# Start bytes of the on-chip buffers in a fused attention, mixing and channel kernel

## The chip, the cores and the metric

The kernel runs on one core of a Trainium2 chip, as one program. The metric is the device time of one execution in microseconds (us). The engines are TensorE (PE, with its weight loads PEld), VectorE (DVE), ScalarE (ACT), GpSimd (POOL) and the queue of SyncE (SP), which issues all DMAs.

## The reference

Three stages follow each other, with batch 4, 576 positions and 512 channels.

```
attention: 8 heads of 64; heads 0-3 see a window of 32, heads 4-7 every 4th of 128 positions
x  = softmax(mask(q k^T / 8)) v                          # (4, 576, 512)
xk = mu_k x + (1 - mu_k) x_prev;  xr = mu_r x + (1 - mu_r) x_prev   # x_prev: one position back
y  = sigmoid(xr w_r) * (relu(xk w_k)^2 w_v)              # w_k: 512x1024, w_v: 1024x512
u  = y + (y^T U V)^T                                     # U: 576x32, V: 32x576, over positions
out = u + relu(u w_ch1) w_ch2                            # w_ch1: 512x2048, w_ch2: 2048x512
```

## The kernel before

All products of the second and third stage are made with channels on the 128 partitions. A float32 operand is split in two (`hi_lo`, `part_split`): ACT copies it rounded into a high half, DVE or POOL subtracts to get the low half. A product is then a trio of float32r matmuls: high weights times high data, low weights times high data, high weights times low data. In a matmul the first operand named in a row of the profile is the one that streams through the array (the moving operand), the second is the one that is loaded before it (the stationary operand, here always the weights).

**Mixing stage.** The 2304 positions are cut into 8 chunks of 288 columns (`HS`). Chunk 0 uses plain float32 matmuls (lines 1101 and 1116) while the weights still come in. Chunks 1 to 7 use trios (lines 1088 to 1090), with data in the tiles `xk` (tag `A`) and `k2s` (tag `B`) and weights in pieces of 128x512 (tag `w`, 42 of them, names `wh` and `wl`). Attention for later chunks runs between them: small matmuls (lines 848, 913, 949, 1005), softmax on DVE, ACT and POOL with the small tiles `mn` and `sm` (tags with 3 buffers), and `x_out`, which writes the attention's output into tile `x`, one row of 577 columns for each of four channel blocks (column 0 holds a zero, for `x_prev`).

**Channel stage.** From about 332 us on, the last two products run in groups of 512 columns by a seven-product scheme (`ch1`, `ch2`), in blocks of 256 columns (`Q`). Old tiles get new tenants ("boxes"): the data `u` and its sums stand in the tags `w64` and `raw` (profile names `boxw` and `boxraw`), the hidden values' high halves in `B`, `raw` and the end of `x`, their low halves in the two buffers of `x`: `x[0]` for even steps `j`, `x[1]` for odd ones. The weights of three steps in four (`j % 4 < 3`) stand in pieces of tag `w`, those of the fourth in the boxes `A` and `B`. Matmuls of `ch1` are lines 1365 to 1367, those of `ch2` lines 1453 to 1455. DVE makes the sums, the low halves, the weights' sums for later steps and the stores' sums.

**Order.** Each engine's order comes from a planner (`plan`): it walks over all operations by fixed ranks (`RANKS`) and assumed durations, and lets an operation that opens a new buffer of a tag wait for the buffer's previous tenant (`x.bufs`). The order is fixed when the program is built.

**Where the buffers lie.** `Lazy` asks the pool for a tile when an operation first uses it. A pool gives each tag one stretch, in the order of first use; each buffer of a tag is rounded up to a multiple of 32 bytes. The small pool `cp` starts at a multiple of 128 bytes, with `cst_t` (1792 bytes in each partition), `mu_t` (32) and `zero` (2048); the big pool follows. So the start bytes, modulo 128, are:

| tag, in order | buffers x bytes | starts at byte (of 128) |
|---|---|---|
| raw | 4 x 5120 | 32 |
| x | 2 x 9232 (9248) | 32 and 64 |
| w64 | 4 x 4096 | 96 |
| pr | 4 x 2560 | 96 |
| mn, sm | 3 x 20 (32) each | 96, 0, 32; 64, 96, 0 |
| w32 | 3 x 2048 | 32 |
| w | 42 x 2048 | 32 |
| pt, d, sig, rt, B, m, A, y, k2, us, vs | all multiples of 128 | 32 |

A chunk's 288 columns take 1152 bytes, a block's 256 columns 1024 bytes: both are multiples of 128, so each operand inside a tile starts at the same byte of 128 as its tile. In tile `x` a row takes 2308 bytes, so its four rows start 4 bytes apart.

Of the kernel before, what the change touches and what calls it, by code (L numbers as in the profile page):

```python
# [12 lines left out]
F32 = mybir.dt.float32  # L13
# [7 lines left out]
B, H, S, D = 4, 8, 576, 64  # L21
DM, DFF, DCH, RANK = 512, 1024, 2048, 32
P = 128
HS = S // 2
NCH = 2 * B
NPAIR = H // 2
# [25 lines left out]

NPIECE = 42
XW = 16 * HS

CLAMP = 400
END_ENG = ("ACT",) * 8 + ("DVE",)
# [146 lines left out]
def tile_attention_mix_channel(  # L204
# [4 lines left out]
    cp = ctx.enter_context(tc.tile_pool(name="cp", bufs=1))  # L209
    pool = ctx.enter_context(tc.tile_pool(name="pool", bufs=2))  # L210
# [4 lines left out]
    cst_t = cp.tile([P, P + NALL * KW], F32, name="cst_t")  # L215
    ident = cst_t[:, 0:P]
    masks = [cst_t[:, P + i * KW : P + (i + 1) * KW] for i in range(NALL)]
    mu_t = cp.tile([P, 8], F32, name="mu_t")
    zero = cp.tile([P, CW], F32R, name="zero")

    def f32(ap):
# [1 line left out]


    ops = []

    class Lazy:

# [5 lines left out]
        def __call__(self):  # L234
            if self.real is None:
                shape, dt, name = self.args
                self.real = self.home.tile(shape, dt, tag=self.tag, name=name, bufs=self.bufs)
            return self.real

    def bank(tag):  # L240

        return Lazy([P, 512], F32, tag, f"ps{tag}", 4, ps)
# [4 lines left out]
    def op(eng, ns, fn, r=(), w=(), more=100, lock=False, mode=None, size=0):  # L247

        o = Op()
        o.eng, o.ns, o.fn, o.r, o.w, o.more, o.lock, o.mode, o.size = eng, ns, fn, list(r), list(w), more, lock, mode, size  # L250
        ops.append(o)
# [227 lines left out]
    def dma(nbytes, fn, r, w):  # L479
        op("SP", 415, fn, r, w, size=nbytes)  # L480
# [13 lines left out]
    def copy(n, out_, in_, r, w, psum=False, strided=False):  # L494
        act(n, lambda: nc.scalar.activation(out_(), in_(), AF.Copy), r, w, psum, strided)  # L495
# [244 lines left out]
    xt = {}  # L740
    raws = {}

    def unit(u):
        part_i, pair = divmod(u, NPAIR)
        b, part = divmod(part_i, 2)
        return b, part, pair
# [65 lines left out]
    def x_out(ov, q, part, b):  # L812

        if b not in xt:
            xt[b] = Lazy([P, NPAIR, S + 1], F32, "x", f"x{b}", 2)
            op("POOL", 105, lambda: nc.gpsimd.memset(xt[b]()[:, :, 0:1], 0.0), [], [(xt[b], "z")])
        t0, t1 = PARTS[part]

        def dst():
            d = xt[b]()[:, q, 1 + t0 : 1 + t1]  # L820
            return d.rearrange("p (m r) -> p r m", r=DIL) if q >= NPAIR // 2 else d

        def src():
            s_ = ov()[:, : t1 - t0]
            return s_.rearrange("p (r m) -> p r m", r=DIL) if q >= NPAIR // 2 else s_

        copy(t1 - t0, dst, src, [(ov,)], [(xt[b], q, part)], psum=True, strided=q >= NPAIR // 2)

    def attend(u):
# [3 lines left out]
        b, part, pair = unit(u)  # L833
# [1 line left out]
        raw = raws.pop(u)  # L835
        sc = [bank("M" if u < SC_M else "S") for _ in range(2)]
        pr = Lazy([P, 10 * KW], F32, "pr", "pr", 4)
        mn, sm = Lazy([P, 5], F32, "mn", "mn", 3), Lazy([P, 5], F32, "sm", "sm", 3)
        pt, ov = bank("S"), bank("S")
        pts = Lazy([P, 5 * P], F32, "pt", "pts", 2)  # L840

# [76 lines left out]
        pe(nw * 4, nw * 2 * 66, pv, [(pts, 0), (raw, "v")], [(ov,)], "pv")  # L918
        yield
        x_out(ov, pair, part, b)  # L920
        yield

    def attend2(ua, ub):
# [4 lines left out]
        b, part, pair = unit(ua)  # L928
# [1 line left out]
        rq, rv = raws.pop(("qk", ua // 2)), raws.pop(("v", ua // 2))  # L930
        sc = [bank("S") for _ in range(2)]
        pr = Lazy([P, 10 * KW], F32, "pr", "pr", 4)
        mn = [Lazy([P, 5], F32, "mn", "mn", 3) for _ in range(2)]
        sm = [Lazy([P, 5], F32, "sm", "sm", 3) for _ in range(2)]
        pt, ov = bank("S"), [bank("S") for _ in range(2)]
        pts = Lazy([P, 5 * P], F32, "pt", "pts", 2)
        ns = nw // 2
# [74 lines left out]
        for x in range(2):  # L1012
            x_out(ov[x], pair + x, part, b)
# [36 lines left out]
    k20 = Lazy([P, 8 * HS], F32, "B", "k20", 1)  # L1050
    xk = Lazy([P, XW], F32R, "A", "xk", 1)
    k2s = Lazy([P, XW], F32R, "B", "k2s", 1)

# [143 lines left out]
    yb = {}  # L1197
# [3 lines left out]
    uacc = {}  # L1201

    def load_y(b):
        yb[b] = Lazy([P, NPAIR, S + 1], F32, "x", "yb", 2)
        dma(P * S * 16, lambda: nc.sync.dma_start(yb[b]()[:, :, :S], ytmp[b]),
            [("y", b, o, h) for o in range(4) for h in range(2)], [(yb[b],)])

# [377 lines left out]
    def fresh(n):  # L1585

        nonlocal nunit
        us_ = range(nunit, min(nunit + n, NU))
        nunit += len(us_)
        for d in (0, 2):  # L1590
            for what in ("qk", "v"):
                for u in us_ if d == 0 or nunit > NPAIR else ():
                    fetch(u + d, what)
        return [attend2(*us_)] if len(us_) == 2 else [attend(u) for u in us_]
# [33 lines left out]
    for p in range(NPAIR):  # L1628
        mix(0, p, "k")
    divided = 0  # L1630
    side = [lambda: load_y(0)] + uv_u(0, "S", "S") + uv_v(0, "S") + uv_v(1, "S") + [lambda: load_y(1)]
    side += uv_u(1, "S", "S") + uv_v(2, "S") + uv_v(3, "S")
    side += [lambda: load_y(2)] + uv_u(2, "S", "S") + uv_v(4, "S") + uv_v(5, "S")
    for c in range(NCH - 1):
        cur = quanta(c) if c else first
# [34 lines left out]
    for n, (g, j0, j1) in enumerate(VISITS):  # L1670
        boxes.pop(("sig", 0), None)
        nxt = x_steps(VISITS[n + 1][0]) if n + 1 < len(VISITS) else []
        todo = [lambda: load_y(3)] + uv_u(3, "S", "S") + uv_v(6, "S") + uv_v(7, "S") if n == 0 else []
        each = (len(todo) + 3) // 4
        for j in range(j0, j1):
            hid = ch1(g, j)
            for what in LATER.get((n, j), ()):
                prep(*what)
            if PRESUM <= 4 * n + j < PRESUM + 8:
                presum(4 + (4 * n + j - PRESUM) // 2, 1 + (4 * n + j - PRESUM) % 2)  # L1680
            for _ in range(each):
                if todo:
                    todo.pop(0)()
            if prev is not None:
                ch2(*prev)
            prev = (g, j, hid, j == j0, j == j1 - 1, (j0 == 0, j1 == 8))
            for fn in nxt[:1] if j == (j0 if j1 - j0 == 4 else j1 - 2) else nxt[1:] if j == j1 - 1 else ():
                fn()
# [106 lines left out]
```

## Time and profile before

| | |
|---|---|
| median of 3 runs | 725.76 us (725.61 to 726.69) |
| profiled execution | 726.45 us, of which the span from first to last instruction is 724.6 us |
| PE busy | 715.0 us (99%) |
| DVE busy | 596.3 us (82%) |
| ACT busy | 422.8 us (58%) |
| POOL busy | 128.1 us (18%) |
| PE's share of the chain that ended last | 89% |

Busy is the time in which at least one instruction of an engine runs, waits inside PE's pipeline included, so a busy PE isn't one at its peak. The chain that ended last is followed back from the last instruction, at each step to what released it.

### The profile page before, as it was taken

The numbers are of one execution on the slowest core, as the hardware profiler recorded it, in microseconds if no ns is written. First come the engines' busy times: TensorE is split into PE (matmuls) and PEld (weight loads), VectorE is DVE, ScalarE is ACT, GpSimd is POOL, SyncE is SP. The second block draws the span as 40 slices with busy tenths as digits, with TensorE's granted clock in tenths as the row PEclk, the third lists the DMA queues.
The fourth block names the chain that finished last, engine by engine and source line by source line (L and its number), as shares of the span: only waits on it lengthen the run. The fifth ranks groups of instructions, "written<-read, shape, count | busy, mean of one in ns | idle before, by whom it ended". The sixth has DMA issues, their size and how long they took to land.

```text
span 724.6 us, 19178 instructions
## 1 busy us (share of the span) xinstructions
PE 715.0 (99%) x7534; PEld 692.9 (96%) x7534; DVE 596.3 (82%) x1526; ACT 422.8 (58%) x1047; POOL 128.1 (18%) x164
## 2 busy tenths in 40 slices
PE   8999999999999999999899999999999999999997
PEld 6778999999999999999899999999999999999997
DVE  5879988687767645899998999999999898897853
ACT  5887886867676835275643544445586445444321
POOL 0101364646463724130000000000000000000000
PEclk9999999999999999999999999999999999999999
DMA  8986257676647430756546446442554213103221
GB/s 318 350 276 233 83 190 264 234 265 229 233 149 265 156 122 1 252 171 210 188 125 205 142 144 209 153 140 74 164 185 133 59 57 119 30 31 118 88 73 59
DMA packets 69979, 117.71 MB, mean 162 GB/s; under 512 B 6144, under 2 KB 41216, under 8 KB 69888
## 3 DMA queue, kind: packets, MB, share of 16 engines
q1 hardware_dynamic: 69888, 116.49, 48.6%
q8 instruction: 59, 0.97, 0.6%
q14 instruction: 32, 0.26, 0.1%
HBM read 85.00 MB, written 31.46 MB: 161 GB/s over the span
## 4 chain that ended last, share of the span: by engine, by line
PE 89%; DVE 5%; DMA 2%; ACT 2%; issue 1%; SPq 0%; DVEq 0%; ACTq 0%
PE psM L1088 10%; PE psM L1090 10%; PE psM L1089 10%; PE psM L1365 8%; PE psM L1367 7%; PE psM L1366 7%; PE psM L1116 4%; PE psS L1453 4%; PE psS L1455 4%; PE psS L1454 4%; PE psM L1455 3%; PE psM L1453 3%; PE psM L1454 3%; PE psS L1005 2%; PE psS L949 2%; PE psM L1101 1%
## 5 line engine op out<-in xcount | busy, mean ns | idle before, releaser
L1088 PE MATMUL psM<-xk,wh 128*128 128x288 f32 x336 | 101.0, 301 | 0.0
L1089 PE MATMUL psM<-xk,wl 128*128 128x288 f32 x336 | 99.2, 295 | 0.0
L1090 PE MATMUL psM<-xk,wh 128*128 128x288 f32 x336 | 99.0, 295 | 0.0
L1088 PE MATMUL psM<-k2s,wh 128*128 128x288 f32 x224 | 67.4, 301 | 0.0
L1089 PE MATMUL psM<-k2s,wl 128*128 128x288 f32 x224 | 66.1, 295 | 0.0
L1090 PE MATMUL psM<-k2s,wh 128*128 128x288 f32 x224 | 66.0, 295 | 0.0
L1088 PEld LDWEIGHTS psM<-xk,wh 128*128 128x128 f32 x336 | 63.1, 188 | 0.8
L1089 PEld LDWEIGHTS psM<-xk,wl 128*128 128x128 f32 x336 | 63.2, 188 | 0.2
L1090 PEld LDWEIGHTS psM<-xk,wh 128*128 128x128 f32 x336 | 63.3, 188 | 0.0
L1365 PE MATMUL psM<-boxraw,wh 128*128 128x256 f32 x198 | 56.5, 285 | 0.5 <-ACT hc L1435 0.5
L1367 PE MATMUL psM<-boxraw,wh 128*128 128x256 f32 x198 | 56.0, 283 | 0.0
L1366 PE MATMUL psM<-boxraw,wl 128*128 128x256 f32 x198 | 56.0, 283 | 0.0
L1455 PE MATMUL psS<-boxx,wh 128*128 128x256 f32 x192 | 54.4, 283 | 0.0
L490 POOL TENSOR_TENSOR k2s<-k,k2s 128x288 fp32r<-128x288 f32 x49 | 43.2, 885 | 62.7 <-ACT k2s L495 23.7
L1365 PE MATMUL psM<-boxw,wh 128*128 128x256 f32 x186 | 52.5, 282 | 0.2 <-DVE hb L1415 0.2
L1367 PE MATMUL psM<-boxw,wh 128*128 128x256 f32 x186 | 51.9, 279 | 0.3 <-DVE boxw L492 0.3
L1366 PE MATMUL psM<-boxw,wl 128*128 128x256 f32 x186 | 51.8, 279 | 0.0
L782 ACT ACTIVATE pr<-pr,mn 128x64 f32<-128x64 f32 x144 | 48.0, 335 | 5.1 <-DVE mn L773 4.9
L490 POOL TENSOR_TENSOR xk<-m,xk 128x288 fp32r<-128x288 f32 x48 | 42.9, 901 | 36.9 <-ACT xk L495 22.8
L1164 DVE SCALAR_TENSOR_TENSOR k<-psM,rt 128x288 f32<-128x288 f32 x56 | 25.1, 454 | 22.2 <-ACT rt L1159 18.5
L1088 PEld LDWEIGHTS psM<-k2s,wh 128*128 128x128 f32 x224 | 42.1, 188 | 0.6
L1089 PEld LDWEIGHTS psM<-k2s,wl 128*128 128x128 f32 x224 | 42.1, 188 | 0.2
(255 smaller groups left out, 2491.1 us busy)
## 6 DMA issues: line engine op xcount, KB each, us to landing
w<-w2raw SPq DMA_DIRECT2D x32, 512.0 KB, 5.5
w<-w1raw SPq DMA_DIRECT2D x20, 512.0 KB, 6.7
w2f<-w SPq DMA_DIRECT2D x32, 256.0 KB, 3.2
ub<-uf SPq DMA_DIRECT2D x32, 256.0 KB, 3.1
ws<-w2f SPq DMA_DIRECT2D x24, 256.0 KB, 4.2
raw<-qk SPq DMA_DIRECT2D x16, 320.0 KB, 6.8
ytmp<-y SPq DMA_DIRECT2D x32, 144.0 KB, 2.7
yb<-ytmp SPq DMA_DIRECT2D x4, 1152.0 KB, 6.9
```

Source lines behind the costliest of these rows:

```text
L490: op("POOL", t, lambda: nc.gpsimd.tensor_tensor(out=out_(), in0=a(), in1=b(), op=ALU.subtract), r, w, 40, lock=True)
L782: nc.scalar.activation(pr[:, d : d + KW], pr[:, d : d + KW], AF.Exp, bias=mn[:, i : i + 1], scale=-1.0, accum_out=sm[:, i : i + 1])
L1088: nc.tensor.matmul(a, lhsT=wh, rhs=xh, start=start, stop=False)
L1089: nc.tensor.matmul(a, lhsT=wl, rhs=xh, start=False, stop=False)
L1090: nc.tensor.matmul(a, lhsT=wh, rhs=xl, start=False, stop=stop)
L1116: pe(2, MM1, lambda o=o, acc=accs[o]: nc.tensor.matmul(acc()[:, :HS], lhsT=whole_w[w]()[:, o * P : (o + 1) * P], rhs=cols(src, n), start=f ...
L1365: nc.tensor.matmul(a, lhsT=wh(*wi), rhs=xh(*ci), start=start and n == 1, stop=False, skip_group_check=True)
L1366: nc.tensor.matmul(a, lhsT=wl(*wi), rhs=xh(*ci), start=False, stop=False, skip_group_check=True)
L1367: nc.tensor.matmul(a, lhsT=wh(*wi), rhs=xl(*ci), start=False, stop=last, skip_group_check=True)
L1453: nc.tensor.matmul(a, lhsT=wh(*wi), rhs=xh(), start=start, stop=False, skip_group_check=True)
L1454: nc.tensor.matmul(a, lhsT=wl(*wi), rhs=xh(), start=False, stop=False, skip_group_check=True)
L1455: nc.tensor.matmul(a, lhsT=wh(*wi), rhs=xl(), start=False, stop=stop, skip_group_check=True)
```

## The change

Nothing of the arithmetic changes. `mu_t` takes 96 bytes in place of 32, so that all that follows moves by 64 bytes. A row of `x` gets 584 columns, of which 577 are used, so that one buffer of `x` takes 9344 bytes (73 times 128) and its rows start 32 bytes apart. The tags `mn` and `sm` get four buffers of 32 bytes in place of three. Two unused tiles of 64 bytes are put ahead of the first piece of tag `w` and ahead of the first tile of tag `pt`. By the sizes above, every tag from `raw` on, both buffers of `x` included, then starts at byte 96 of 128; only the 42 pieces of `w` start at byte 32, as before.

```diff
+XCOLS = 584
-    mu_t = cp.tile([P, 8], F32, name="mu_t")
+    mu_t = cp.tile([P, 24], F32, name="mu_t")[:, :8]
+    PADS = ['w', 'pt']
@@ Lazy.__call__
             if self.real is None:
                 shape, dt, name = self.args
+                if self.home is pool and self.tag in PADS:
+                    PADS.remove(self.tag)
+                    pool.tile([P, 16], F32, tag=f"pad{self.tag}", name=f"pad{self.tag}", bufs=1)
                 self.real = self.home.tile(shape, dt, tag=self.tag, name=name, bufs=self.bufs)
@@ x_out
-            xt[b] = Lazy([P, NPAIR, S + 1], F32, "x", f"x{b}", 2)
+            xt[b] = Lazy([P, NPAIR, XCOLS], F32, "x", f"x{b}", 2)
@@ attend (attend2 likewise, two of each)
-        mn, sm = Lazy([P, 5], F32, "mn", "mn", 3), Lazy([P, 5], F32, "sm", "sm", 3)
+        mn, sm = Lazy([P, 5], F32, "mn", "mn", 4), Lazy([P, 5], F32, "sm", "sm", 4)
@@ load_y
-        yb[b] = Lazy([P, NPAIR, S + 1], F32, "x", "yb", 2)
+        yb[b] = Lazy([P, NPAIR, XCOLS], F32, "x", "yb", 2)
```

## Rows read from the trace of the kernel before

**Rows 1.** Page: span, busy time by engine, and the chain that ended last.
```profile
span 724.6 us, 19178 instructions
PE 715.0 (99%) x7534; PEld 692.9 (96%) x7534; DVE 596.3 (82%) x1526; ACT 422.8 (58%) x1047; POOL 128.1 (18%) x164
PE 89%; DVE 5%; DMA 2%; ACT 2%; issue 1%; SPq 0%; DVEq 0%; ACTq 0%
```

**Rows 2.** Windows: stretch, its length, busy us of each engine (instructions), PE clock, DMA.
```profile
80.00:332.00 252.00, 252.00 (x3349) 247.55 (x3347) 189.80 (x590) 167.49 (x486) 119.78 (x148) 1.00 0.57 192
332.00:380.00 48.00, 45.70 (x347) 43.06 (x346) 46.67 (x99) 27.50 (x53) 0.00 (x0) 1.00 0.52 169
400.00:560.00 160.00, 159.60 (x1339) 159.06 (x1338) 152.65 (x317) 87.12 (x171) 0.00 (x0) 1.00 0.47 149
...
400.00:420.00 20.00, 20.00 (x171) 20.00 (x170) 19.59 (x42) 11.38 (x24) 0.00 (x0) 1.00 0.41 130
520.00:540.00 20.00, 20.00 (x171) 20.00 (x170) 19.88 (x42) 17.16 (x35) 0.00 (x0) 1.00 0.69 213
```

**Rows 3.** Groups by line and form, PE: how many matmuls of each operand.
```profile
L1088 PE MATMUL psM<-xk,wh 128*128 128x288 f32 x336 | 101.0, 301 | 0.0
L1088 PE MATMUL psM<-k2s,wh 128*128 128x288 f32 x224 | 67.4, 301 | 0.0
L1365 PE MATMUL psM<-boxraw,wh 128*128 128x256 f32 x198 | 56.5, 285 | 0.5 <-ACT hc L1435 0.5
L1365 PE MATMUL psM<-boxw,wh 128*128 128x256 f32 x186 | 52.5, 282 | 0.2 <-DVE hb L1415 0.2
L1365 PE MATMUL psM<-boxraw,boxA 128*128 128x256 f32 x66 | 18.8, 284 | 0.0
L1365 PE MATMUL psM<-boxw,boxA 128*128 128x256 f32 x62 | 17.6, 283 | 0.4 <-DVE hb L1415 0.4
```

**Rows 4.** Windows of line 1453 alone (the first two), and of line 1365 (the last).
```profile
332.00:724.60 392.60, 144.73 (x512) 97.75 (x512) 1.00 0.39 122
...
332.00:380.00 48.00, 9.13 (x32) 6.08 (x32) 1.00 0.52 169
...
332.00:380.00 48.00, 12.84 (x45) 8.49 (x45) 1.00 0.52 169
```

**Rows 5.** Timeline, PE, moving at byte 32: first and last of 12, and of 72.
```profile
440.12 0.28 PE L1365 MATMUL psM<-boxraw,boxA 128*128 128x256 f32 x1
...
441.44 0.28 PE L1367 MATMUL psM<-boxraw,boxA 128*128 128x256 f32 x1
...
709.24 0.28 PE L1453 MATMUL psS<-boxB,wh 128*128 128x256 f32 x1
...
717.76 0.28 PE L1455 MATMUL psM<-boxB,wh 128*128 128x256 f32 x1
```

**Rows 6.** Timeline, PE: 12 with moving at byte 96, behind a matmul at byte 32.
```profile
667.23 0.28 PE L1455 MATMUL psM<-boxx,wh 128*128 128x256 f32 x1
667.35 0.28 PE L1365 MATMUL psM<-boxw,wh 128*128 128x256 f32 x1
...
668.65 0.28 PE L1367 MATMUL psM<-boxw,wh 128*128 128x256 f32 x1
```

**Rows 7.** Timeline, PE: 12 more at byte 96, behind one at byte 64.
```profile
657.68 0.28 PE L1455 MATMUL psS<-boxx,boxA 128*128 128x256 f32 x1
657.80 0.28 PE L1365 MATMUL psM<-boxw,wh 128*128 128x256 f32 x1
...
659.05 0.28 PE L1367 MATMUL psM<-boxw,wh 128*128 128x256 f32 x1
```

**Rows 8.** Timeline, PE: a step into byte 64; 12 at byte 64.
```profile
450.64 0.29 PE L1455 MATMUL psM<-boxx,boxB 128*128 128x256 f32 x1
450.77 0.28 PE L1453 MATMUL psS<-boxx,wh 128*128 128x256 f32 x1
...
453.26 0.28 PE L1453 MATMUL psM<-boxx,boxB 128*128 128x256 f32 x1
...
454.56 0.28 PE L1455 MATMUL psS<-boxx,boxB 128*128 128x256 f32 x1
```

**Rows 9.** Timeline, PE: 288 columns at byte 32, first and last of 155.
```profile
260.37 0.29 PE L1089 MATMUL psM<-k2s,wl 128*128 128x288 f32 x1
...
280.88 0.29 PE L1090 MATMUL psM<-xk,wh 128*128 128x288 f32 x1
```

**Rows 10.** Groups by line and form, DVE and ACT: like operations on tiles at different bytes.
```profile
L492 DVE TENSOR_TENSOR boxraw<-tt,boxraw 128x512 fp32r<-128x512 f32 x16 | 11.0, 687 | 0.5 <-ACT boxraw L495 0.4
L492 DVE TENSOR_TENSOR boxw<-tt,boxw 128x512 fp32r<-128x512 f32 x14 | 9.6, 686 | 0.1
...
L495 ACT ACTIVATE boxx<-ha 128x512 fp32r<-128x512 f32 x32 | 20.1, 628 | 31.4 <-DVE ha L651 23.7 <-PE psS L1454 7.6
L495 ACT ACTIVATE boxB<-hc 128x512 fp32r<-128x512 f32 x32 | 20.1, 627 | 7.6 <-DVE hc L651 4.6 <-PE psS L1454 2.9
```

**Rows 11.** Tile yb: duration min/median/max of its sums on DVE; its load.
```profile
L1257 DVE TENSOR_TENSOR us<-psS,yb x32: 445/449/459, 293.8 to 377.6; 128x288 f32<-128x288 f32 x32
...
  DMA yb<-ytmp: 2.5, 2
...
DMA to landing us min/median/max: 6.3/6.9/8.7
```

**Rows 12.** Tiles mn and sm: all who waited for them (us, times).
```profile
  POOL pr L799: 5.3, 2
  DVE sm L787: 5.1, 7
  ACT pr L782: 4.9, 4
  POOL d L490: 0.7, 1
...
  POOL pr L799: 19.1, 8
  POOL xk L490: 0.5, 1
```

**Rows 13.** Groups by line and form, PE: attention's matmuls from chunk 1 on.
```profile
L1005 PE MATMUL psS<-pts,raw 64*64 64x32 f32 x992 | 17.3, 220 | 0.0
...
L949 PE MATMUL psS<-raw 64*32 64x64 f32 x992 | 13.4, 224 | 0.0
```

More of the change, by code (lines that the diff above doesn't have):

```diff
@@ L932, in attend2 @@
         pr = Lazy([P, 10 * KW], F32, "pr", "pr", 4)
-        mn = [Lazy([P, 5], F32, "mn", "mn", 3) for _ in range(2)]
-        sm = [Lazy([P, 5], F32, "sm", "sm", 3) for _ in range(2)]
+        mn = [Lazy([P, 5], F32, "mn", "mn", 4) for _ in range(2)]
+        sm = [Lazy([P, 5], F32, "sm", "sm", 4) for _ in range(2)]
         pt, ov = bank("S"), [bank("S") for _ in range(2)]
```

## The prediction

> **What bounds the kernel now.** I read the page's busy times and its chain first [rows 1]: PE is busy for 99% of the span, 89% of the chain that ended last is PE, so the time is the sum of the steps from the start of one matmul to the next. The windows by stage [rows 2] say where that holds. From 80 to 332 us (mixing) PE never pauses, DVE has a quarter of the time free. From 332 to 380 us DVE is busy for 46.67 of 48 us and PE pauses for 2.3: there DVE sets the pace. From 400 us on PE hardly pauses again (0.4 us to 560), but DVE has only 7.35 of 160 us free, and almost nothing in 400 to 420 and 520 to 540.
>
> A change of addresses alters no instruction, so the question is whether an instruction's time depends on the byte at which its operands start. I took the matmuls' starts from the timeline and sorted them by the start byte of the moving operand, which the table of buffers gives.
>
> Weights start at byte 32 throughout. With the moving operand at byte 32 as well, 71 steps take 8.52 us and 11 steps on `raw` take 1.32, 120.0 ns each [rows 5]. At byte 96, 11 steps take 1.30 us, 118.2 ns [rows 6], or 1.25 us, 113.6 ns [rows 7]. At byte 64, 11 steps take 1.30 us, 118.2 ns [rows 8]. So the byte matters. The two paces at byte 96 are a choice made on entry and kept: of the 82 stretches of 6 or more, 59 go at about 118 and 23 at about 113.3. Of those 23, 21 come right behind a matmul at byte 64, as in [rows 7]; of the 49 that come behind any other byte, 47 go at 118, as in [rows 6]. The fast 23 hold 210 of the 3 x (186 + 62) = 744 matmuls at byte 96 [rows 3].
>
> With 288 columns the trace has byte 32 alone: 154 steps take 20.51 us, 133.2 ns [rows 9]. That is 13.2 ns over 120.0 for 32 more columns, the time of 32 cycles at the granted 2.4 GHz (clock 1.00 in [rows 2]). So the part that isn't columns is the same at both widths, and I let it shrink alike.
>
> **The change part by part.** By the sizes, afterwards all moving operands start at byte 96, and the weights in pieces of `w` at byte 32: the pair of [rows 6]. Byte 64, the way into the fast pace, is gone. So I price a step at 118.0 ns, the nearest rows; the other ends are 113.3 (all fast) and 120.0 (no change).
>
> (a) Mixing: 336 + 224 matmuls in each of three lines [rows 3], 1680, by 133.2 - 131.2 = 2.0 ns: 3.4 us gained.
> (b) Channel stage, `ch1`, data in `raw`, weights in `w`: 3 x 198 = 594 by 2.0: 1.2 us.
> (c) `ch2`: 3 x 512 = 1536 [rows 4], of which three steps in four have weights in `w`: 1152 by 2.0: 2.3 us. Trios that mix bytes 32 and 64 I count at 120 too: what the step into byte 64 loses, the step out of it gives back.
> (d) `ch1`, data in `w64`: already at byte 96. The 210 that now go at 113.3 lose their way in: 210 by 4.7: 1.0 us lost.
> (e) Every fourth step's weights lie in `A` and `B` and move to byte 96 with the data. No row has weights off byte 32. If the distance between the two operands counts, both at one byte is the case of [rows 5], 120.0: nothing for 198 + 384 matmuls, and the 186 of `boxw` with `boxA` [rows 3] lose 2.0, 0.4 us. If the moving operand's byte alone counts, 582 gain 2.0, 1.2 us. I take the middle, 0.4 us gained.
>
> Sum: 3.4 + 1.2 + 2.3 - 1.0 + 0.4 = 6.3 us.
>
> The Trainium skill's page "TensorE: Matmul & The Clock Gate" (Part 2, What happens when you issue a matmul) gives PE two independent read ports to on-chip memory, so that loading the next weights takes nothing from the running matmul. By it the weights' byte shouldn't matter, (e) would give 1.2 and the sum would be 7.1; no row here has weights at two bytes, so the trace neither bears it out nor speaks against it.
>
> From this goes what PE can't use. In 332 to 380 us DVE sets the pace; 3 x (32 + 45) = 231 matmuls of the channel stage start there [rows 4], by 2.0: 0.5 us. In the two stretches of 20 us where DVE is nearly full [rows 2], 342 by 2.0 is 0.7, of which DVE has 0.5 free: about 0.3 lost. Net: 6.3 - 0.8 = 5.5 us.
>
> **What costs nothing.** Nobody waits for a free buffer of `mn` or `sm`: `mn` is first written by DVE on line 773 and `sm` by ACT on line 782, and among those who waited for these tiles [rows 12] there is no line 773, and line 782 only for `mn`, which it reads. So the fourth buffer frees nothing, and I expect the planner, which knows the same waits, to find the same order. If it didn't, the longest of these waits are of some 5 us in 7 pieces: under a microsecond each, either way. DVE and ACT don't mind the byte: `boxraw` at 32 and `boxw` at 96 take 687 and 686 ns, `boxx` and `boxB` 628 and 627 [rows 10]; sums that read `yb` at eight different bytes lie between 445 and 459 ns [rows 11]. So the wider rows of `x` are worth nothing to them. The load of `yb` lands in 6.3 to 8.7 us into either buffer [rows 11]; what waited for it directly is 2.5 us in all, so rows on 32-byte steps could give at most that, and as the landing shows no pattern I take nothing. Attention's matmuls have both operands in tiles that move together by 64 bytes, and no row shows them elsewhere. They hold PE for 17.3 + 13.4 us [rows 13]; by the 1.7% of the others (2.0 of 120.0) that is at most 0.5 us either way, and I take nothing. Chunk 0's float32 matmuls lie beside loads and I take nothing there either.
>
> So the profiled execution's 726.45 us (span 724.6 and 1.85 around it) becomes 720.95. It lies 0.7 above the median of the runs, 725.76, which becomes **720.3 us**. From the bounds of (e) and of DVE's share alone: 718 to 722.
>
> **The rivals.**
>
> *The fast pace for all.* If streams that stay at byte 96 fall into the 113.3 ns pace (two of the 49 did so without byte 64, and none that had it left it within its 6 or 12 matmuls), (a) gives 1680 x 6.7 = 11.3, (b) and (c) 1746 x 6.7 = 11.7, (d) 348 x 4.7 = 1.6: 24.6. DVE then takes part back: 231 x 6.7 = 1.5 in 332 to 380, and in 400 to 560 PE would save some 6.5 us where DVE has 7.35 free in scattered pieces; I lose 3 there. About 20 us, 706. If half of the stream is fast, about 713. Against it: after a pause PE comes back at 118.
>
> *Nothing happens.* The pace at byte 96 could belong to what `ch1` does with `w64`, or to other engines that leave that byte alone today and will share it afterwards. Then 725.8, or 726.8 with (d)'s loss. For it: only one tag stands at 96 among PE's data. Against it: the same lines 1365 to 1367 run at 120.0 on `raw`, and byte 64 differs from 32 on a tile far from `w64` [rows 5, 8]. The Trainium skill's page "SBUF — State Buffer" (Specifications (TRN2)) speaks for it: it has lines of 16 bytes, and bytes 32 and 96 both begin one, so by it a step would stay at 120.0 and the time at 725.8. By that rule the trace doesn't agree: [rows 5] and [rows 6] differ by 1.8 ns.
>
> *Slower.* The 288-column matmuls have no row off byte 32. The price that speaks against them is the first step into byte 64, which takes some 123 ns by the timeline's starts (0.13 us in [rows 8], shown to 0.01) and not 120. If 288 columns at byte 96 pay 3.3 ns each instead of gaining 2.0, (a) turns from +3.4 to -5.5, and the whole to 729.2. It decides from 2.1 ns lost per matmul on: the other terms leave 2.1 us, 0.2% (about what a measurement of this kernel can tell from no change) is 1.4, and 3.5 us over 1680 are 2.1 ns. Against it: the extra time beside the columns is equal at both widths.
>
> **How the numbers follow.** Forecast (718 to 723.5): 0.50. Fast pace for much of the stream (below 718): 0.27. Nothing: 0.16. Slower: 0.07. The likeliest is 720.3. For 8 in 10 the range takes in the half-fast case and no change, and leaves out the fully fast case and the slower one: 711 to 726. Faster by over 0.2% 0.77, within it 0.16, slower 0.07.
>
> **What would show it.** The page's groups for `xk` and `k2s` keep their counts and a long run of 288 columns steps at 131 ns, not 133.2. Runs on `raw`, `B` and both buffers of `x` step at 118, and the two buffers no longer differ. Steps with weights in `boxA` tell (e): 120 by distance, 118 by the moving operand alone. DVE's busy time in us stays, its share rises, and idle of PE behind DVE grows in 400 to 440 and 520 to 540. DVE, ACT and POOL keep their mean ns. Wrong would be: an unchanged 133.2, or 113 in long runs, or an order that differs.

## The result, and the profile after

The changed kernel takes 720.75 us, the median of 4 runs (719.02 to 722.05); the kernel before took 725.75 beside it. The ratio is 0.9913, with a 95% interval from 0.9887 to 0.9938. The forecast was 720.3 in 711 to 726. The profiled execution took 722.05 us, 4.40 less than that of before.

The page of the changed kernel, its span, its busy times and the chain that ended last, beside [rows 1]:

```profile
span 720.3 us, 19185 instructions
PE 709.9 (99%) x7534; PEld 687.5 (95%) x7534; DVE 596.8 (83%) x1526; ACT 422.2 (59%) x1047; POOL 127.7 (18%) x164
PE 89%; DVE 5%; DMA 3%; issue 1%; ACT 1%; SPq 0%; DVEq 0%
```

PE has 5.1 us less work with the same 7534 matmuls; DVE, ACT and POOL stay within 0.6 us. The order of instructions is the same on every engine. So the time came from the steps of PE, as forecast. The timeline of PE after, at the same instructions as [rows 9] and the second pair of [rows 5] (lines are numbered 6 higher):

```profile
259.50 0.29 PE L1095 MATMUL psM<-k2s,wl 128*128 128x288 f32 x1
...
279.86 0.30 PE L1096 MATMUL psM<-xk,wh 128*128 128x288 f32 x1
...
705.00 0.28 PE L1459 MATMUL psS<-boxB,wh 128*128 128x256 f32 x1
...
713.37 0.28 PE L1461 MATMUL psM<-boxB,wh 128*128 128x256 f32 x1
```

154 steps of 288 columns take 20.36 us, 132.2 ns each and not 133.2. 71 steps of 256 columns take 8.37, 117.9 ns and not 120.0. Sorting all starts as the prediction did, and leaving out the steps that hold a pause (over 160 ns), gives its terms as they came out:

```
term                              matmuls   ns before   ns after   us gained   predicted
(a) mixing, 288 columns             1680      133.1       132.3       1.4         3.4
(b) ch1, raw, weights in w           594      119.6       116.0       2.1         1.2
(c) ch2, weights in w               1152      119.6       117.4       2.5         2.3
(d) ch1, w64, weights in w           558      116.6       115.9       0.4        -1.0
(e) weights in A and B               767      119.2       118.5       0.6         0.4
sum                                                                   6.9         6.3
all other steps (pauses, clock)                                      -2.5        -0.8
```

Where the 2.5 us went is in the windows. Of the changed kernel (columns as in [rows 2]):

```profile
332.00:380.00 48.00, 45.89 (x341) 43.20 (x340) 46.25 (x96) 26.89 (x53) 0.00 (x0) 0.96 0.52 165
...
380.00:716.00 336.00, 333.95 (x2839) 333.06 (x2838) 294.70 (x604) 164.39 (x317) 0.00 (x0) 1.00 0.37 116
...
348.00:350.00 2.00, 1.19 (x5) 0.75 (x6) 2.00 (x5) 0.37 (x1) 0.00 (x0) 0.86 0.96 251
350.00:352.00 2.00, 2.00 (x8) 1.62 (x7) 0.95 (x3) 1.06 (x2) 0.00 (x0) 0.50 1.02 357
352.00:354.00 2.00, 2.00 (x12) 1.68 (x11) 2.00 (x7) 1.91 (x5) 0.00 (x0) 0.78 1.09 386
...
348.00:356.00 8.00, 7.19 (x39) 6.05 (x40) 6.87 (x16) 5.34 (x11) 0.00 (x0) 0.79 0.83 272
```

Of the kernel before, the same view:

```profile
380.00:716.00 336.00, 335.07 (x2805) 334.11 (x2805) 295.14 (x603) 164.83 (x317) 0.00 (x0) 1.00 0.37 116
...
348.00:350.00 2.00, 0.99 (x5) 0.33 (x3) 2.00 (x6) 1.57 (x3) 0.00 (x0) 1.00 1.02 349
350.00:352.00 2.00, 1.18 (x7) 1.07 (x8) 1.30 (x3) 0.49 (x1) 0.00 (x0) 1.00 0.95 289
```

From 380 us on PE now pauses 2.05 us, before 0.93: 1.1 us more, of which 0.9 is one wait, shown below. In 332 to 380 it pauses about as long as before (2.1 and 2.3 us), but its clock falls: 0.86, 0.50, 0.78 in three windows of 2 us, and 0.50 of full speed is 1.2 GHz. At 0.79 over 8 us, 1.7 us of work are lost. What ran there, from the timeline of the changed kernel:

```profile
342.98 0.69 PE L1255 MATMUL psS<-vs,g 128*128 128x288 f32 x4
...
347.82 0.73 PE L1707 MATMUL psS<-zero 128*128 128x512 f32 x2 [0.88 <-DVE us L1263]
349.37 1.08 PE L1220 MATMUL psS<-cst_t,yb 128*128 128x128 f32 x4 [0.81 <-DMA yb<-ytmp]
350.10 2.90 PE L1707 MATMUL psS<-zero 128*128 128x512 f32 x6
352.80 0.43 PE L1238 MATMUL psS<-yh,us 128*128 128x512 f32 x1
```

and of the kernel before:

```profile
344.22 0.69 PE L1249 MATMUL psS<-vs,g 128*128 128x288 f32 x4
...
349.06 0.73 PE L1701 MATMUL psS<-zero 128*128 128x512 f32 x2 [0.80 <-DVE us L1257]
350.82 0.66 PE L1214 MATMUL psS<-cst_t,yb 128*128 128x128 f32 x4 [1.02 <-DMA yb<-ytmp]
351.23 1.63 PE L1701 MATMUL psS<-zero 128*128 128x512 f32 x6
352.70 0.40 PE L1232 MATMUL psS<-yh,us 128*128 128x512 f32 x1
```

The changed kernel comes to the first of these instructions 1.24 us earlier and to the last 0.10 later: after two waits, six matmuls on zeros take 2.90 us in place of 1.63, and all that the mixing had gained is gone. Such a drop is not in every run. Of the ten traces of whole kernels, three have it at this place, with 1.7 us of work lost in each (this one, e8_distances and e9_mixing_64). Two others have the same distances as the changed kernel and no drop; in that of e5_three_buffers the same six matmuls take:

```profile
349.46 1.64 PE L1707 MATMUL psS<-zero 128*128 128x512 f32 x6
```

The four runs of the changed kernel have mean clocks of 0.998, 0.999, 1.000 and 1.000 and take 722.05, 721.64, 719.86 and 719.02 us. How much of that spread is the drop isn't shown: the kernel before, run beside e1_grid, takes 724.95 to 729.05 us at mean clocks of 0.999 and 1.000.

The wait behind 380 us, in the changed kernel and then in the kernel before: DVE waits for a load, works on almost without a break, and PE waits for what it makes.

```profile
441.38 0.43 DVE L657 TENSOR_TENSOR ps<-ps 128x256 f32<-128x256 f32 x1 [1.47 <-DMA ps<-w2f]
...
445.69 0.39 PE L1371 MATMUL psM<-boxw,boxA 128*128 128x256 f32 x1 [1.28 <-DVE hb L1421]
...
441.74 0.43 DVE L651 TENSOR_TENSOR ps<-ps 128x256 f32<-128x256 f32 x1 [0.66 <-DMA ps<-w2f]
...
446.05 0.39 PE L1365 MATMUL psM<-boxw,boxA 128*128 128x256 f32 x1 [0.38 <-DVE hb L1415]
```

In e5_three_buffers the same two waits are 0.57 and 0.38 us. So neither loss has to come with these distances.

### The profile page after: what moved, and what is told of

It is laid out like the page before. It is cut to its first block, busy times and chain, and to the rows that moved or that the text cites. A ratio compares the mean times of both kernels' runs of the same rounds, so it can differ in the third digit from the quotient of the medians.

```text
span 720.3 us, 19185 instructions
## 1 busy us (share of the span) xinstructions
PE 709.9 (99%) x7534; PEld 687.5 (95%) x7534; DVE 596.8 (83%) x1526; ACT 422.2 (59%) x1047; POOL 127.7 (18%) x164
## 4 chain that ended last, share of the span: by engine, by line
PE 89%; DVE 5%; DMA 3%; issue 1%; ACT 1%; SPq 0%; DVEq 0%
PE psM L1094 10%; PE psM L1095 10%; PE psM L1096 10%; PE psM L1371 7%; PE psM L1372 7%; PE psM L1373 7%; PE psM L1122 4%; PE psS L1459 4%; PE psS L1460 4%; PE psS L1461 4%; PE psM L1460 4%; PE psM L1461 4%; PE psM L1459 3%; PE psS L1011 2%; PE psS L955 2%; PE psM L1107 1%
```

## The experiments

The question is what about the two bytes makes a step shorter. The rivals: the **distance** of the two operands' start bytes; the **moving byte** alone; the **neighbours**, other engines at the same byte; and for the two paces, the **way in**.

**Matmuls alone, 8 bytes by 4 (e1_grid).** The core, shortened:

```diff
+for n in (256, 288):
+    for order in (1, -1):
+        for sb in (0, 32, 64, 96)[::order]:
+            for mb in (0, 16, 32, 48, 64, 80, 96, 112)[::order]:
+                for _ in range(4): twelve(mb, sb, n)   # 4 trios
```

> A kernel of its own that leaves out the whole computation: PE runs the trios of the channel stage (two tiles of weights, two of data, float32r) in stretches of 48 matmuls, one stretch for each of 8 start bytes of the moving operand (0 to 112) with each of 4 start bytes of the weights (0, 32, 64, 96), with 256 and with 288 columns, and the whole list twice, the second time backwards; no other engine works meanwhile. At the end it enters byte 96 from byte 32, 64 and 96. Distance theory (the two operands' bytes modulo 128 must differ): 120.0 ns (133.2 with 288 columns) in the four stretches with equal bytes, 118 or less in the other 28. Moving-byte theory: 120.0 wherever the data start at byte 32, 118 or less at byte 96, the same for all four bytes of the weights. Neighbours theory (the byte matters only through what other engines touch): one step in all 32. The prediction took 2.0 ns off at both widths; the trace of the changed kernel shows 0.9 at 288 columns, so this also says whether 288 columns gain less by themselves. If the way into byte 96 sets the fast pace, stretches entered from byte 64 go at 113 and those entered from byte 32 at 118.

Mean step in ns, first and second pass, 256 columns, the first trio of each stretch left out; the rows of 16 and 112, not shown, lie between 117.6 and 118.0:

```
moving   weights 0        32               64               96
  0    116.7 117.7    118.3 118.5    117.8 117.8    117.7 118.6
 32    118.6 118.6    119.6 119.6    117.1 117.2    117.9 117.8
 48    117.8 117.7    117.9 117.8    117.8 117.9    120.1 119.7
 64    117.8 117.8    118.3 118.4    117.7 117.9    118.5 118.4
 80    120.1 119.7    117.8 115.6    117.8 117.8    117.6 117.8
 96    118.5 118.4    117.9 117.8    117.8 118.6    119.6 119.6
```

There are differences with no other engine at work, so the neighbours fall. Byte 32 is slow with weights at 32 and not with weights at 64 or 96, so the moving byte alone falls. But the distance modulo 128 doesn't hold either: 0 on 0 and 64 on 64 are as fast as the rest, and 48 on 96 is slow. The tiles' addresses sort it: modulo **256** the pairs 32 on 32 and 96 on 96 are 128 apart, 0 on 0 and 64 on 64 are 0 apart, and 48 on 96 and 80 on 0 are both 208 apart, with the same steps. With 288 columns the steps lie between 130 and 133.5, and 32 on 32 and 96 on 96, at 131.1 and 132.2, are not among the longest. All entries into byte 96 at the end went at 117.3 to 117.9, none at 113.3; in this kernel the two moving operands of a trio lie 128 apart modulo 256, which turned out not to be the case of most trios in the channel stage.

**All at byte 96 (e2_all96).**

```diff
-    PADS = ['w', 'pt']
+    PADS = []
```

> The changed kernel without the two pads, so that the pieces of w lie at byte 96 like everything else: both operands of every mixing and channel matmul at one byte. Distance theory: every matmul back at 120.0 and 133.2, the whole gain gone, 725 to 726 us. Moving-byte theory: the data are still at byte 96, so 720 to 721 us as with the pads. The trace of the changed kernel has 653 steps with both operands at byte 96 at 118.4 ns, between the two theories: if this is what such steps cost, some 723 us.

**The bytes change places (e3_swap).**

```diff
-    mu_t = cp.tile([P, 24], F32, name="mu_t")[:, :8]
+    mu_t = cp.tile([P, 8], F32, name="mu_t")[:, :8]
```

> The changed kernel with the constants' tile back at 8 columns, so that all buffers lie at byte 32 as before and the two pads put the pieces of w alone at byte 96: the two bytes change places. Distance theory: 96 against 32 is as good as 32 against 96, 720 to 721 us. Moving-byte theory: the data are at byte 32 as before the change, 725 to 726 us (726.8 with the lost fast pace on w64).

All at 96: 727.01 us (12 runs), ratio to before 1.0006, interval 0.9991 to 1.0020; everything is gone. As this run keeps the wider rows of `x` and the fourth buffers, these are worth nothing by themselves. Changed places: 720.70 us, ratio 0.9919 (0.9903 to 0.9935), as the changed kernel. The stretch of [rows 9] in the timeline of the kernel with all at 96:

```profile
262.89 0.29 PE L1095 MATMUL psM<-k2s,wl 128*128 128x288 f32 x1
...
283.41 0.29 PE L1096 MATMUL psM<-xk,wh 128*128 128x288 f32 x1
```

and of the kernel with the bytes changed:

```profile
260.18 0.29 PE L1095 MATMUL psM<-k2s,wl 128*128 128x288 f32 x1
...
280.54 0.30 PE L1096 MATMUL psM<-xk,wh 128*128 128x288 f32 x1
```

20.52 us as before (20.51), and 20.36 as after. The distance counts; the moving byte alone is refuted from both sides. (Modulo 256 the second edit moves all buffers by 64 bytes alike, so each distance is just that of the changed kernel.) The Trainium skill's page "TensorE: Matmul & The Clock Gate" (Part 2, What happens when you issue a matmul) gives PE two independent read ports, from which the prediction took that the weights' byte shouldn't matter. Here that doesn't hold: modulo 128, all at 96 differs from the changed kernel in the byte of the pieces of `w` alone, and is 6 us slower.

**Each distance by itself (e4_distance).** As in e1_grid (the core, shortened), with both weights of a trio at 0 and both moving operands at d modulo 256, as in most trios of the channel stage (160 of 1023 mix two distances), and four orders:

```diff
+at = m0 + d // 4 + (i % 2) * 1024
+xh, xl = m[:, at : at + n], m[:, at + 512 : at + 512 + n]
```

> Again matmuls alone, the computation left out: trios whose two tiles of weights start at 0 modulo 256 and whose two moving operands start at d modulo 256, d from 0 to 240 in steps of 16 bytes, 72 matmuls in a stretch, the 16 distances in four different orders, with 256 and then with 288 columns. In the trace of the changed kernel trios at distance 0 and 128 take 118.5 ns each matmul, at 64 it is 117.7 and at 192 it is 116.1, with 288 columns 132.2 and 132.4; before it was 119.7 and 133.2 at 0 or 128. If the distance alone sets the pace: the same pace in all four stretches of a distance, slow at 0 and 128. If the pace is chosen on entry and kept: stretches of one distance differ, 113.3 and 118 side by side, whatever the distance. If distance and entry both count: each distance has its own small set of paces.

Mean steps in ns, the four orders beside each other where they differ by over 0.5 (the first stretch of all, with the warm-up, left out):

```
d     256 columns                   288 columns
  0   120.0                         131.6
 16   118.7 116.7 113.3 118.7       130.0 131.7 130.0 131.6
 32   116.7                         133.3
 48   118.4                         132.5
 64   113.3 117.8 117.8 117.8       132.2 131.7 131.7 132.2
 80   120.0 120.0 119.9 118.4       131.1
 96   120.0                         131.7
112   113.3 113.3 113.6 113.7       134.6 134.6 133.3 133.2
128   118.6 118.7 118.7 120.0       133.3
144   118.8 118.7 118.7 113.3       130.0 130.0 130.0 131.1
160   117.3                         133.3
176   119.2                         131.4
192   117.8 113.3 113.6 117.8       133.3
208   119.1                         133.3
224   118.3                         133.3
240   117.2                         131.9
```

The timeline of this kernel, the first and the last matmul of a stretch of 72 at 112, of one at 192 entered from 176, and of one at 192 entered from 112:

```profile
87.52 0.28 PE L35 MATMUL ps<-m,s 128*128 128x256 f32 x1
...
95.57 0.28 PE L37 MATMUL ps<-m,s 128*128 128x256 f32 x1
...
129.79 0.28 PE L35 MATMUL ps<-m,s 128*128 128x256 f32 x1
...
138.15 0.28 PE L37 MATMUL ps<-m,s 128*128 128x256 f32 x1
...
206.01 0.28 PE L35 MATMUL ps<-m,s 128*128 128x256 f32 x1
...
214.06 0.28 PE L37 MATMUL ps<-m,s 128*128 128x256 f32 x1
```

71 steps take 8.05, 8.36 and 8.05 us: 113.4, 117.8 and 113.4 ns. Each distance has a pace of its own or a choice of two, so distance and way in both count. With weights in `w`, the changed kernel stands at 64 (`B`, one buffer of `x`) and 192 (`raw`, `w64`, the other buffer), where both paces are to be had; the kernel before stood at 0, for one buffer of `x` at 32, and for `w64` at 64. With 256 columns, only 112 came to 113.3 from each of its four ways in.

**Three buffers for mn and sm (e5_three_buffers).**

```diff
-    mn, sm = Lazy([P, 5], F32, "mn", "mn", 4), Lazy([P, 5], F32, "sm", "sm", 4)
+    mn, sm = Lazy([P, 5], F32, "mn", "mn", 3), Lazy([P, 5], F32, "sm", "sm", 3)
-    PADS = ['w', 'pt']
+    PADS = ['w', 'pt', 'w32']
```

> The changed kernel with mn and sm back in three buffers each and one more pad of 64 bytes, which keeps every other buffer at its byte. If the fourth buffers only move addresses, as the prediction has it: the same order of instructions and the time of the changed kernel, 720 to 721 us. If the fourth buffer frees a wait in the attention: up to a microsecond lost.

720.98 us, ratio 0.9931 (0.9912 to 0.9950), same order: the fourth buffers only move addresses.

**The mixing's turns, and bytes between (e6_mixed_distance).** As e4_distance, with `(i % 2) * 128` added to d for 288 columns, then d = 8, 24, ... 248 for 256.

> Matmuls alone once more, the computation left out. First 288 columns with trios by turns at distance d and d + 128 modulo 256, as the mixing's data lie (their steps are 1152 bytes), d from 0 to 120 in steps of 8; then 256 columns at d = 8, 24, ... 248, each place in four orders. From the distances measured one by one (288 columns: 131.6 at 0 and 133.3 at 128; 130.0 to 131.7 at 16 and 130.0 at 144; 131.7 to 132.2 at 64 and 133.3 at 192), the mean of the two for d = 0 is 132.5, for 16 it is 130.0 to 130.8, for 64 it is 132.5 to 132.8. If the mean of the two holds, 16 is the best place for the mixing by some 2 ns; if each trio starts anew from the one before, 0 comes out near 133.2 as in the kernel before. The 256-column stretches say whether 113.3 at 112 is one point or a stretch of distances.

By turns 0 and 128 give 133.2 to 133.3, 64 and 192 give 132.2, 16 and 144 give 131.6. These are the mixing's steps in the kernel before (133.2) and after (132.2) to 0.1 ns, so the 288 columns gain 1.0 by themselves. The mean of the two single paces holds at none of the three (132.5 for 0; 132.5 to 132.8 for 64; 130.0 to 130.8 for 16). With 256 columns at odd multiples of 8, 50 of the 64 stretches go at 119.9 to 120.2; those at 72 and 216 and some at 8, 120 and 136 lie between 116.7 and 122.7, one at 104, entered from 88, stays at 129.4, and 113.3 is in none, not even at 104 or 120. The Trainium skill's page "SBUF — State Buffer" (Specifications (TRN2)) has lines of 16 bytes. By it a start inside a line is another case than a start on one, and the trace agrees. That two starts on lines cost the same, as the rival "nothing happens" had it, the trace refutes (113.3 to 120.0 in the table).

**w at byte 0 (e7_w_at_0).**

```diff
-                    pool.tile([P, 16], F32, tag=f"pad{self.tag}", name=f"pad{self.tag}", bufs=1)
+                    pool.tile([P, 8 if self.tag == 'w' else 24], F32, tag=f"pad{self.tag}", name=f"pad{self.tag}", bufs=1)
```

> The changed kernel with the pad ahead of w cut to 32 bytes and the one behind raised to 96, so that the pieces of w start at byte 0 and all else stays at 96. If it is enough that the two bytes differ: 720 to 721 us, as with w at 32. If the distance modulo 256 sets the pace as in the runs of matmuls alone: w64 and raw lie at 224 from their weights (118.35 instead of 113.3 to 117.8), boxB and one buffer of x at 96 (120.0), together some 2 ns more than the 116.7 of the changed kernel on 2300 matmuls, 5 us of which DVE hides about 1; the mixing at 96 and 224 (131.65 and 133.33, mean 132.5 beside 132.3) stays within 0.5 us: 724 to 725 us.

724.12 us, ratio 0.9971 (0.9959 to 0.9984): as the table has it. Bytes that merely differ are not enough. The timeline, the 71 steps on `boxB`, now 96 from `wh`:

```profile
707.22 0.28 PE L1459 MATMUL psS<-boxB,wh 128*128 128x256 f32 x1
...
715.73 0.28 PE L1461 MATMUL psM<-boxB,wh 128*128 128x256 f32 x1
```

8.51 us, 119.9 ns, with operands at bytes 96 and 0.

**Bytes from the table (e8_distances), and the mixing back (e9_mixing_64).** A part of a box may start some columns in, `XW` tiles are 32 columns wider, and the pads and the boxes' sizes are set anew (not shown):

```diff
+    SKIP = {("raw", 2): 44, ("raw", 3): 44, ("x", 0): 44, ("x", 1): 52, ("A", 0): 32, ("sig", 0): 28}
-        return Part(boxes[tag, i], unit * Q, n * Q)
+        return Part(boxes[tag, i], unit * Q, n * Q, SKIP.get((tag, i), 28 if tag == "B" and unit >= 10 else 0))
-        return t()[:, n * HS : (n + 1) * HS]
+        at = n * HS + (4 if t in (xk, k2s) else 0)   # e9_mixing_64: 16
+        return t()[:, at : at + HS]
```

> The changed kernel with the bytes chosen from the runs of matmuls alone, the order of the instructions as before: the weights in A and B moved to the same byte modulo 256 as the pieces of w, the channel stage's data in B, x, sig and two of the four raw buffers at distance 112 from their weights (113.3 in all four orders), the full buffers (two of raw, w64) at 192, and xk and k2s at 16 and 144 (131.64 by turns). By the table of distances: channel matmuls at 112 fall from 117 to 118.5 to 113.3, some 600 trios by about 4 ns each matmul, 7.5 us; the weights of A and B under w64 and raw go from distance 0 to 192, 0.8 us; the mixing falls from 132.3 to 131.6, 1.1 us. 9.4 in all, of which DVE takes back some 3: 713 to 715 us, faster than the changed kernel. If the paces found without other engines at work do not hold beside DVE and ACT: 719 to 722 us. If 16 bytes off a step of 32 cost DVE, ACT or the transfers something: their mean ns rise and the gain is smaller by it.

> The same kernel with xk and k2s back at distance 64 and 192 from their weights, as in the changed kernel, and the channel stage as in the run beside it. By the table: the mixing at 132.3 in place of 131.6, 1680 matmuls by 0.65, so 1.1 us more than the run beside it; all that remains below the changed kernel's 720.8 is the channel stage's.

718.82 us (ratio 0.9906, 0.9888 to 0.9924) and 719.38 (0.9919, 0.9895 to 0.9943): the mixing's part points the right way, but within the spread; in the two traces its 1680 steps differ by 1.0 us, as expected. The channel stage gave far less than expected. The timeline of e8_distances shows why, at the first matmul of each trio around a step from `w64` (192) to `boxB` (112):

```profile
647.79 0.28 PE L1374 MATMUL psM<-boxw,wh 128*128 128x256 f32 x1
...
648.13 0.29 PE L1462 MATMUL psM<-boxB,wh 128*128 128x256 f32 x1
...
648.51 0.28 PE L1462 MATMUL psM<-boxx,boxB 128*128 128x256 f32 x1
...
648.86 0.28 PE L1462 MATMUL psS<-boxB,wh 128*128 128x256 f32 x1
...
649.21 0.28 PE L1374 MATMUL psM<-boxraw,wh 128*128 128x256 f32 x1
...
649.57 0.28 PE L1374 MATMUL psM<-boxraw,wh 128*128 128x256 f32 x1
...
649.90 0.28 PE L1374 MATMUL psM<-boxraw,wh 128*128 128x256 f32 x1
```

The first trio at the new distance takes 0.38 us (125 ns a matmul), three more 0.35 or 0.36, and only the fifth 0.33 to 0.34, which is 113.3. Of the stretches at one distance, 322 of 356 are shorter than five trios, and the trios at 112 take 117.7 ns a matmul on average. A change of distance itself costs.

**One distance (e10_one_distance), and the ways in (e11_entry).** The first edit is shown against e8_distances, without the sizes and the mixing's offsets, which keep 16 and 144.

```diff
-    SKIP = {("raw", 2): 44, ("raw", 3): 44, ("x", 0): 44, ("x", 1): 52, ("A", 0): 32, ("sig", 0): 28}
+    SKIP = {("x", 1): 32, ("A", 0): 16, ("sig", 0): 48}      # all at 192; B: 48 from unit 10 on
```

> The changed kernel with every channel trio at one distance, 192 modulo 256: the weights of A and B at the byte of the pieces of w, data in B, sig and one buffer of x moved inside their boxes; xk and k2s at 16 and 144 as in the run before last, order of instructions unchanged. In the kernel with 112 and 192 mixed the first trio after a step from 192 to 112 took 125 ns each matmul, the next ones 117 and 118, and 113.3 only came with the fifth. If changes of distance cost the pace: with none left, trios at 192 keep nearer to 113.3; at 115 in place of the 117.4 that kernel shows over both distances, 3070 matmuls give 7 us, of which DVE takes perhaps half, 715 to 716 us. If the distance alone sets the pace: 192 with its two paces of 113.3 and 117.8 is no better than 112, 718 to 720 us.

718.42 us, ratio 0.9888 (0.9859 to 0.9917): no better than 112 and 192 mixed. Nearly all trios go at 113.3 (about 250) or at 117.8 (about 720). Only the two settled paces are left, but the slow one settles three times as often; the mean is 116.7, where that of e8_distances is 116.8 (and not 117.4, as the expectation has it).

The core of e11_entry, shortened:

```diff
+for to in (64, 192):
+    for before in range(0, 256, 32):
+        twelve(before, 256)
+        for _ in range(6): twelve(to, 256)
+for one, other in ((192, 192), (192, 112), (192, 64), (64, 0), (192, 128)):
+    for _ in range(16): twelve(one, 256); twelve(other, 256)
```

> Matmuls alone, the computation left out, 256 columns. First 72 matmuls at distance 64, and then at 192, each entered from 12 matmuls at one of the 8 distances 0, 32, ... 224. Then 16 turns of 12 matmuls at one distance and 12 at another: 192 and 192, 192 and 112, 192 and 64, 64 and 0, 192 and 128. If the way in sets the pace, as the prediction took from the rows behind byte 64: entered from 32 the stretch at 64 goes at 113.3, entered from 0 or 128 at 117.8, and by turns the mean lies above both settled paces. If not: one pace whatever came before, and the turns give the mean of the two distances.

Into 192 from 0, 32, 64, 96 or 128 PE goes at 113.3 from the third trio at the latest; from 160 or 224 it stays at 117.8. The timeline: 72 at 192 entered from 128, and 468 at 192 entered from 224.

```profile
146.58 0.28 PE L32 MATMUL ps<-m,s 128*128 128x256 f32 x1
...
154.65 0.28 PE L34 MATMUL ps<-m,s 128*128 128x256 f32 x1
...
175.96 0.28 PE L32 MATMUL ps<-m,s 128*128 128x256 f32 x1
...
230.97 0.28 PE L34 MATMUL ps<-m,s 128*128 128x256 f32 x1
```

8.07 us for 71 steps, 113.7 with the way in; 55.01 for 467, 117.8 to the end. This slow stretch does not speed up by itself. Into 64 all eight ways gave 117.8, also that from 32, so the part of the expectation on the kernel before's way in is refuted here. By turns, 192 and 192 take 117.8 (the slow pace), 192 and 112 take 116.7, 192 and 64 take 115.8, 192 and 128 take 117.2, 64 and 0 take 119.1. That the mean by turns lies above both settled paces, as expected, holds at most for 192 and 112.

**All at 112 (e12_all_112).** The pads, the boxes' sizes and the reading of the smaller tile of zeros are not shown.

```diff
-    zero = cp.tile([P, CW], F32R, name="zero")
+    zero = cp.tile([P, P], F32R, name="zero")
+    SKIP = {("raw", 0): 12, ("raw", 1): 4, ("raw", 2): 52, ("raw", 3): 28, ("w64", 0): 28, ("w64", 1): 44,
+            ("w64", 2): 36, ("w64", 3): 52, ("x", 0): 44, ("x", 1): 52, ("A", 0): 32, ("sig", 0): 28}
```

> The changed kernel with every channel trio at distance 112 modulo 256, the one that ended at 113.3 from every way in, and the mixing at 16 and 144. To make room for 16-byte steps inside the full buffers of raw and w64 the tile of zeros is cut from 512 to 128 columns and read several times over by the filling matmuls, which multiply zeros as before; order of instructions unchanged. With one distance of 192 some 720 of 986 trios stayed at 117.8 all through and 240 at 113.3, mean 116.7. If 112 settles at 113.3 from any start in about four trios, also after a pause, and some 30 pauses are left: 120 trios at 118 and the rest at 113.4, mean 114.0, 2.7 ns less on 2960 matmuls, 8 us, of which DVE, with some 5 us free from 400 to 560 us in scattered pieces, takes about 3: 713 to 714 us. If beside DVE and ACT 112 has a slow pace of its own as well: 717 to 719 us.

713.19 us (712.64 to 713.77), ratio **0.9821** (0.9805 to 0.9838): the fastest of all. Its page, windows and timeline:

```profile
span 710.8 us, 19185 instructions
PE 700.7 (99%) x7534; PEld 677.6 (95%) x7534; DVE 595.5 (84%) x1526; ACT 422.3 (59%) x1047; POOL 127.4 (18%) x164
```

```profile
332.00:380.00 48.00, 45.60 (x349) 42.73 (x348) 47.59 (x101) 27.98 (x55) 0.00 (x0) 1.00 0.55 173
400.00:560.00 160.00, 158.91 (x1375) 157.73 (x1373) 154.87 (x325) 88.04 (x173) 0.00 (x0) 1.00 0.48 149
```

```profile
696.06 0.28 PE L1462 MATMUL psS<-boxB,wh 128*128 128x256 f32 x1
...
704.11 0.28 PE L1464 MATMUL psM<-boxB,wh 128*128 128x256 f32 x1
```

The 71 steps take 8.05 us, 113.4 ns; of some 980 channel trios that have no pause in them, some 800 go at 113, and every stretch of five trios or more is there by the fifth. After a short stall (a trio at 127 to 131 ns) it mostly begins anew, with two trios at about 118 and one at 115. From 400 to 560 us 1375 matmuls fit where 1339 did [rows 2]. ACT's and DVE's busy times show no price of steps of 16 bytes.

## Why the prediction came out right

**What bounds the kernel, and the sign: right.** PE's step was the bound, the step hangs on the bytes, and the order of instructions did not change. All at 96 takes the whole gain away.

**The price of 118.0 ns: read at another distance.** In [rows 6] the data lie 64 from their weights modulo 256. Afterwards `B` and one buffer of `x` do so too, but `raw`, `w64` and the other buffer of `x` stand at 192, which a table of bytes modulo 128 cannot tell from 64. In the changed kernel steps at 64 take 117.7 ns and steps at 192 take 116.1. The price held for the first; what (b) and (d) brought beyond it is luck.

**(a) Mixing: the mechanism right, the size 2.4 times too large.** The step was that "the part that isn't columns is the same at both widths, and I let it shrink alike". It shrank by 0.9 ns, not 2.0: 1.4 us, not 3.4. Matmuls alone give the same 133.2 and 132.2 by turns. Paces are not columns plus a constant: at distance 112, 256 columns are fastest and 288 columns slowest.

**(b), (c): as forecast or more.** 3.6 ns in place of 2.0 for `raw`, 2.2 for `ch2`. `raw` now stands at 192 and is at 113.3 part of the time: a piece of the rival "fast pace for all".

**(d): wrong in sign.** "Lose their way in" failed. That a pace is chosen on entry and kept is right and was shown; that byte 64 is the way in was an accident of one layout. The step from distance 0 or 128 into 192 does the same, `w64` itself moved from 64 to 192, and it gained 0.4 us where 1.0 lost was forecast.

**(e): right by a middle that neither bound explains.** Distance counts, so the weights that moved along stayed slow beside `w` (118.5), yet they gained 0.6 us; their distances are now 0 and 128. By the traces `boxw` lost 1.0 ns a step (117.3 to 118.3), half of what the distance bound has, and `raw`, from 0 to 128, gained 1.4. `boxB` stays at 0 and gained 1.2 all the same, so something else counts too, perhaps what runs before it; no run tests that on `boxB` alone.

**What DVE takes: 0.8 us forecast, something else seen.** (Its 0.3 for the two full stretches is 0.7 less 0.5, so 0.2.) In the profiled run a clock that fell to 0.50 took up to 1.7 us and a wait behind a late load 0.9; neither is DVE short of time, and neither was in the sum. The traces of e3_swap and e5_three_buffers, at the same distances, gain the same 6.9 us in the steps of (a) to (e) and lose 1.0 and 0.2 elsewhere, and from 380 to 700 us PE pauses 1.0 and 0.4 us in them, before 0.9. So no price of DVE's full stretches shows. That the sum came out at 6.9 for 6.3 and the median 0.45 us from the forecast is partly luck: (a) fell 2.0 short, (b) and (d) brought 2.3 too much, and the losses had other causes than the one forecast.

**The rivals.** Fast pace for all did not come with this change but was there to be had: with all at 112 it gives 713.2, and not 706, since the mixing gains 1.5 ns a step and not 6.7, and four trios pass before the pace is reached. "Nothing" and "slower" are refuted by 1680 steps at 132.3.

**Open.** Why a distance has the paces it has; why in the kernel before 21 of the 33 stretches behind byte 64 (distance 32) were fast, and none in matmuls alone (the prediction's 82 less 49 are these 33; its 21 of 23 leaves out the 12 at 118); and what sets off the drop of the clock.

## What to carry to other kernels

Where PE never pauses, measure its step over the start bytes of both operands before choosing a layout, with the same trios, widths and strides as the kernel's: such a table forecast e7_w_at_0, and with the price of settling also e12_all_112, to within a microsecond, and missed e8_distances by 4 us because changes of distance were not in it. Choose a distance that settled fast from every way in that was tried, and keep to it, for a change of distance can cost some trios. The clock can fall, or a load come late, in one run and not in another; look at the granted clock and the waits of each stretch, in more than one trace, before calling a gain lost.

## What the runs showed of the hardware that was not expected

- The step of a float32r matmul hangs on the distance of its two operands' start addresses modulo 256: 113.3 to 120.0 ns with 256 columns, 130.0 to 134.6 with 288, no other engine at work.
- At some distances (16, 64, 80, 128, 144 and 192 with 256 columns) PE has two or three paces, chosen by what ran before; at 192 it kept the slow one over 467 steps.
- Data that start 8 bytes off a step of 16 go at about 120.0 in 50 of 64 stretches with 256 columns.
- Two waits of 0.7 to 1.0 us, with two matmuls between them, were followed by a granted clock of 0.50 in three traces; in the kernel before, with waits of 0.8 and 1.0 us, the clock stayed at 1.00.
